# Turning q and k by 32 by 32 blocks on VectorE for seven of sixteen head pairs, with another order of the first loads' turns, in a fused BigBird attention and FNet kernel

## The chip, the cores and the metric

The kernel runs on one core of a Trainium2 chip. The metric is the device time of one execution in microseconds (us). TensorE is called PE here, VectorE DVE, ScalarE ACT, GpSimd POOL and SyncE SP, as the profile calls them; PEld is PE's loading of weights.

## What is computed

First comes block-sparse attention over 4 batches of 8 heads, 768 rows, head width 64, in float32. A row attends to its own 32-row block, the two neighbours, the first and last block, and three random blocks. Then, per batch, a Fourier mix and a two-layer network with 512 and 2048 channels:

```python
scores = scale * np.matmul(q, k.transpose(0, 1, 3, 2))     # masked by 32 x 32 blocks
attn = np.exp(scores - max) / sum
x = (attn @ v), heads side by side                          # (4, 768, 512)
mixed = np.real(np.fft.fft(np.fft.fft(x, axis=1), axis=2))
u = x + mixed
un = (u - mean) / np.sqrt(var + 1e-6)
out = u + np.maximum(un @ w_ch1, 0.0) @ w_ch2
```

## The kernel before

**Pairs, units, slots.** Heads are taken two at a time: 16 pairs (`n` = 0 to 15), four per batch. Both heads of a pair lie side by side on the 128 partitions (64 each) once q and k have been turned, so that the head's 64 columns are the contracted dimension. A pair has 12 units: 2 halves of the queries (384 rows each) by 6 tiles of 128 keys. A *slot* holds two units, so a pair has six slots, `s` = 0 to 5, and a batch (a *phase*) 24. `slot` writes down one slot: `scores` of its two units (four matrix products, L478), `weigh` (the exponential on ACT, L497, then the mask product on DVE, L499; in the first batch, phase 0, the mask is added on PE instead, L483, and ACT writes the weights itself, L494), then `values` of the units of the slot before (L522). From the second batch on, POOL adds up the weights (L509) and PE sums them over partitions once a pair (`total`, L583).

**Work of the mixer between the slots.** While batch b+1 is in attention, the Fourier mix and the network of batch b are placed between its slots; those of the last batch come after all slots. The network's first layer is done in `quad` (seven products of four matrix products each, L898), its second in `channels` (L954, "y" in the profile). The kernel keeps a small model of the time of each engine (`when`, `free`, `busy`, `give`) while it is being built, and `gap` places the next piece where that model says that its inputs are ready. Once it is built the order on every engine is fixed.

**Turning.** `load_q` and `load_k` bring a pair in with the rows on partitions. `turn` turns one half of q or k: PE transposes 128 by 128 pieces into the one PSUM bank of pool `ps_t` ("t"), four then two for q and three then three for k (L447, 12 per pair), and ACT copies them out (L450 for k, six copies and then three for q, L456, which also put q's rows into the order that the Fourier mix wants). At the end ACT squares the raw tile and keeps the sum per partition (L462), from which `highest` later decides whether the safe path `general` must run. The same bank is used by `place` (the transposes `xt`, L540, copied by ACT, L541), by `total`, and by part of the mixer's transposes (`utp`, L823). `slot` appends the turns of pair n+1 to a list `short` at s = 1, 2 (q) and 4, 5 (k); `gap` takes them from it when the model says that they are ready, and a loop near the end of `slot` forces out what is left. Loads are issued on SP's queue: q of pair n+2 at s = 3, k of pair n+1 at s = 0, each into a single buffer.

**The start.** For pair 0 the copies of q's first half are shared between DVE and ACT in turn, those of the second half are DVE's. DVE also builds the mask tables (L232, L245) and rounds the float64 weights of the network to float32, one 512-column chunk at a time, with two ACT operations (L410, L413) and then five DVE operations (L414 to L422) each; `w_steps` asks for 1.42 chunks per slot in phase 0. `warm` issues products of the identity that keep PE running while the first data arrives.

Of the kernel before, what the change touches and what calls it, by code (L numbers as in the profile page):

```python
# [11 lines left out]
FP32 = mybir.dt.float32  # L12
# [6 lines left out]
ACT = mybir.ActivationFunctionType  # L19
# [45 lines left out]
           ((384, 64, 191, 64, 64, -1), (704, -128, 64, 63, 63, -1), (640, 127, 0, 1, 1, 1)))  # L65


def _rows(view, tile):

    got = []  # L70
    for t, p0, runs, jump, n, s0, step in _ORDER:
        if t != tile:
            continue
        at = view[s0:s0 + 1, :]
        row, col = list(at.ap[0])[0], list(at.ap[1])
        if jump > 0:
            got.append((p0, runs * n, bass.AP(tensor=at.tensor, offset=at.offset,
                                              ap=[[jump * row, runs], [step * row, n], col])))
            continue
        for r in range(runs):  # L80
            at = view[s0 + r * jump:s0 + r * jump + 1, :]
            got.append((p0 + r * n, n, bass.AP(tensor=at.tensor, offset=at.offset,
                                               ap=[[step * row, n], col])))
    return got
# [3 lines left out]
def kernel(  # L88
# [14 lines left out]
    nc = tc.nc  # L103

    B, H, S, D = q.shape
    DM = H * D
    FF = w_ch1.shape[1]
    P = 128
    C = S // P
    BLK = 32  # L110
# [10 lines left out]
    scale = 1.0 / float(D) ** 0.5  # L121
    KA = D + NB
    NP = H // 2
    LIMIT = 400.0

    const = ctx.enter_context(tc.tile_pool(name="const", bufs=1))

# [25 lines left out]
    peaks = const.tile([P, 2 * B * NP], FP32, name="peaks")  # L153

    ld = ctx.enter_context(tc.tile_pool(name="ld", bufs=1))
    ldv = ctx.enter_context(tc.tile_pool(name="ldv", bufs=2))
    tp_p = ctx.enter_context(tc.tile_pool(name="tp_p", bufs=2))
# [16 lines left out]
    when = {"PE": 0.0, "ACT": 0.0, "DVE": 0.0, "POOL": 0.0}  # L174
    free = {"m": [0.0, 0.0], "t": [0.0]}

    def busy(engine, us, after=0.0):
        when[engine] = max(when[engine], after) + us
        return when[engine]
# [13 lines left out]
    pairs = [(b, j) for b in range(B) for j in range(NP)]  # L193
    loaded, v_of = {}, {}

    def load_k(n, queue=None):

        b, j = pairs[n]
        kt = loaded.get((n, 1))
        if kt is None:  # L200
            kt = ld.tile([P, C, 2, D], FP32, tag="k", name="kr")
        for i in range(2):
            (queue or nc.sync).dma_start(out=kt[:, :, i, :],
                                         in_=k[b, 2 * j + i].rearrange("(p c) d -> p c d", p=P))
        loaded[n, 1] = kt

    def load_q(n):

        b, j = pairs[n]
        qt = loaded.get((n, 0))  # L210
        if qt is None:
            qt = loaded[n, 0] = ld.tile([P, T, 2, 2, D], FP32, tag="q", name="qr")
        for t in range(T):
            for i in range(2):
                rows = q[b, 2 * j + i][2 * P * t:2 * P * (t + 1), :]
                nc.sync.dma_start(out=qt[:, t, :, i, :],
                                  in_=rows.rearrange("(p r) d -> p r d", r=2))
# [36 lines left out]
    def bit(n):  # L254
# [6 lines left out]
                                  ap=[[0, NB], [1, 2 * NB * NR]]))  # L261
# [3 lines left out]
    def warm(n):  # L265

        m = ps_m.tile([P, P], FP32, tag="m", name="warm")
        for _ in range(n):
            nc.tensor.matmul(m, ident, ident, start=True, stop=True)
# [163 lines left out]
    def turn(n, a, half):  # L433

        t = loaded[n, a]
        if half == 0:
            turned[n, a] = tp_p.tile([P, S], FP32, tag="qk"[a] + "T", name="qk"[a] + "T")
        dst = turned[n, a]
        first = n == 0 and half == 0
        tag, pool = ("m", ps_m) if first and a == 0 else ("t", ps_t)  # L440
        tp, at = pool.tile([P, 512], FP32, tag=tag, name="tp"), bank(tag)
        if a == 0:
            parts = [t[:, c // 2, c % 2, :, :] for c in (range(4, 6) if half else range(4))]
        else:
            parts = [t[:, T * half + c, :, :] for c in range(T)]
        for c, part in enumerate(parts):
            nc.tensor.transpose(tp[:, c * P:(c + 1) * P], part, ident)  # L447
        done = busy("PE", 0.15 * len(parts)) + HOP
        if a == 1:
            nc.scalar.copy(out=dst[:, half * HS:(half + 1) * HS], in_=tp[:, 0:HS])  # L450
            give(at, busy("ACT", 0.5, done))
        else:
            for i, (to, to_jump, frm, jump, cnt, step) in enumerate(_TURNED[half]):
                on, copy = (("DVE", nc.vector.tensor_copy) if n == 0 and (half == 1 or i % 2 == 0)
                            else ("ACT", nc.scalar.copy))
                copy(out=_grid(dst, to, 2, to_jump, cnt, 1),  # L456
                     in_=_grid(tp, frm, 2, jump, cnt, step))
                end = busy(on, 0.27 if cnt > 1 else 0.18, done)
            give(at, end)
        if half == 1:  # L460
            flat = t.rearrange("p t r i d -> p (t r i d)" if a == 0 else "p c i d -> p (c i d)")
            nc.scalar.activation(out=flat, in_=flat, func=ACT.Square,  # L462
                                 accum_out=peaks[:, 2 * n + a:2 * n + a + 1])
            busy("ACT", 1.05)

    UP = 2 * C
    UNITS = len(pairs) * UP
# [709 lines left out]
    def slot(sl):  # L1177
        phase, r = divmod(sl, SB)
        n, s = divmod(sl, SP)
        units = range(SLOT * sl, SLOT * sl + SLOT)  # L1180
        if sl < B * SB:
            for u, ps in [(u, scores(u)) for u in units]:
                weigh(u, ps)
        if not late:
            gap(1.5)
        if 0 < sl <= B * SB:
            done = [u - SLOT for u in units]
            for u in done:
                values(u)
            if phase == 0 or sl == SB:  # L1190
                add_up(done)
            for u in done:
                e_of.pop(u)

        reuse = n % NP == 0 and phase >= 2
        if sl > 0 and s == (5 if reuse else 3) and sl <= B * SB:
            b, j = pairs[n]
            at = oT_at[n, 0]
            if reuse:
                until(lambda: (b - 2, 0) in finished)  # L1200
                at = when["PE"] + LEAVES
            short.append(("t", at, lambda: place(n, 0)))
        if 0 < sl <= B * SB and s == 0 and n % NP != 1:
            short.append(("t", oT_at[n - 1, 1], lambda: place(n - 1, 1)))
        if sl < B * SB and n % NP == 1 and s == 1:
            b = pairs[n - 1][0]
            at = oT_at[n - 1, 1]
            if b >= 2:
                until(lambda: (b - 2, 1) in finished)
                at = when["PE"] + LEAVES  # L1210
            short.append(("t", at, lambda: place(n - 1, 1)))
        if sl > SB and s == 0 and sl <= B * SB:
            short.append(("t", acc_at[n - 1, 1], lambda: total(n - 1)))
        if n + 1 < len(pairs):
            for at, a, half in ((1, 0, 0), (2, 0, 1), (4, 1, 0), (5, 1, 1)):
                if s == at:
                    short.append(("t", 0.0, lambda a=a, half=half: turn(n + 1, a, half)))
            if s == 1:
                load_v(n + 1)
        if sl == 0:  # L1220
            short.append(("t", 0.0, lambda: turn(0, 1, 1)))
        if sl == 1:
            short.append(("t", 0.0, lambda: turn(0, 0, 1)))
        if phase == 0 and 4 <= sl < 4 + 2 * C:
            short.append(("m", 0.0, lambda: mask_step(sl - 4)))
        if r == 1 and 0 < phase:
            begin(phase - 1)
        left = SB * (phase + (0 if r == 0 else 1)) + 1 - sl
        us = sum(step[1] for step in late)
        pace = max(LEAST, min(MOST, (us - COVER) / left)) if left > 0 else MOST  # L1230
        state["owed"] = min(state["owed"], pace) + pace if late else 0.0
        gap(max(state["owed"], 0.0))
        while late and state["owed"] >= late[0][1] / 2:
            state["owed"] -= late[0][1]
            channel_step()
            gap(max(state["owed"], 0.0))

        while short and (s in (2, 5) or len(short) > 1 or phase == 0 or sl == B * SB):
            short.popleft()[2]()
        if s == 3 and n + 2 < len(pairs):  # L1240
            load_q(n + 2)
        if s == 0 and 0 < n < len(pairs) - 1:
            load_k(n + 1)
        w_loads()
        w_steps(sl)
        if sl >= 4 and sl % 2 == 0:
            table_step()
# [21 lines left out]
    state["got"] = 2  # L1269
    turn(0, 1, 0)  # L1270
    turn(0, 0, 0)
    warm(3)
    spread_q(keep_q[0:NB, :], keep)
    w_loads()
    for sl in range(B * SB + 1):
# [112 lines left out]
```

## Time and profile before

| What | Value |
| --- | --- |
| median of 4 runs | 1112.35 us (1110.98 to 1114.01) |
| the profiled execution's own time | 1111.01 us |
| its span | 1109.3 us |
| PE busy | 1067.5 us, 96% of the span |
| DVE busy | 664.7 us, 60% |
| ACT busy | 393.8 us, 36% |
| POOL busy | 274.2 us, 25% |
| mean granted PE clock | 0.994 |

The span is the time from the first to the last instruction in the trace; the execution's own time is 1.7 us more. A share of busy time is a mean over stages that have different limits, so the stages are read one by one. In this profile a product of 32-bit numbers stands as two matrix products, so "s x8" is the four score products of one slot. A timeline gives start, duration, engine, line, output and inputs, number of instructions, and in brackets how long the engine had been idle and what ended that.

The attention of the four batches lies at 9 to 133 us, 133 to 249 us, 249 to 576 us and 576 to 825 us. The last two hold long stretches (about 272 to 447 us and 605 to 703 us) in which the mixer has PE for itself. From 825 us on only the last batch's mixer is left.

### The profile page before, as it was taken

The numbers are of one execution on the slowest core, as the hardware profiler recorded it, in microseconds if no ns is written. First come the engines' busy times: TensorE is split into PE (matmuls) and PEld (weight loads), VectorE is DVE, ScalarE is ACT, GpSimd is POOL, SyncE is SP. The second block draws the span as 40 slices with busy tenths as digits, with TensorE's granted clock in tenths as the row PEclk, the third lists the DMA queues.
The fourth block names the chain that finished last, engine by engine and source line by source line (L and its number), as shares of the span: only waits on it lengthen the run. The fifth ranks groups of instructions, "written<-read, shape, count | busy, mean of one in ns | idle before, by whom it ended". The sixth has DMA issues, their size and how long they took to land.

```text
span 1109.3 us, 12468 instructions
## 1 busy us (share of the span) xinstructions
PE 1067.5 (96%) x4446; PEld 544.6 (49%) x4446; DVE 664.7 (60%) x1216; ACT 393.8 (36%) x818; POOL 274.2 (25%) x302
## 2 busy tenths in 40 slices
PE   8999988998899999999999999999999999999996
PEld 3333333544455545444444555454444555568675
DVE  5888878497754525653459355544356446575563
ACT  6788755555212102353443212244330202120210
POOL 1000088688100001255537000344540000000000
PEclk9999999999999999999999999999999999999999
DMA  7757311011000000211110000111000000100001
GB/s 219 209 176 214 94 50 43 15 45 42 1 1 1 0 1 19 66 32 28 43 29 15 1 0 1 51 50 29 1 1 0 1 1 19 39 1 1 1 16 44
DMA packets 65187, 44.30 MB, mean 40 GB/s; under 512 B 52814, under 2 KB 57948, under 8 KB 65116
## 3 DMA queue, kind: packets, MB, share of 16 engines
q1 hardware_dynamic: 63228, 42.62, 13.7%
q10 hardware_dynamic: 1856, 0.79, 0.3%
q8 instruction: 37, 0.61, 0.2%
q14 instruction: 34, 0.28, 0.1%
q0 software_dynamic: 32, 0.01, 0.0%
HBM read 37.11 MB, written 6.29 MB: 39 GB/s over the span
## 4 chain that ended last, share of the span: by engine, by line
PE 86%; DVE 8%; ACT 3%; issue 2%; POOL 0%; ACTq 0%; DVEq 0%; POOLq 0%
PE y L954 23%; PE z L898 15%; PE s L478 11%; PE o L522 9%; PE yp L898 7%; PE yy L1017 6%; PE xp L898 4%; DVE e L499 2%; PE tp L447 2%; PE zp L711 1%; PE sp L569 1%; PE xt L540 1%; PE zp L682 1%; PE s L483 1%; PE utp L823 1%
## 5 line engine op out<-in xcount | busy, mean ns | idle before, releaser
L509 POOL TENSOR_TENSOR acc<-acc,e 128x384 f32<-128x384 f32 x192 | 198.3, 1066 | 90.6 <-DVE e L499 90.1
L499 DVE TENSOR_TENSOR e<-s,mask 128x768 f32<-128x768 f32 x144 | 131.2, 951 | 78.4 <-ACT s L497 78.0
L478 PE MATMUL s<-qT,kT 64*128 64x384 f32 x768 | 161.6, 526 | 9.3 <-DVE e L499 7.4
L522 PE MATMUL o<-e,vr 128*64 128x384 f32 x768 | 145.1, 499 | 0.0
L497 ACT ACTIVATE s<-s 128x768 f32<-128x768 f32 x144 | 109.2, 794 | 65.4 <-PE s L478 64.6
L957 DVE TENSOR_TENSOR x<-y,x 128x512 f32<-128x512 f32 x72 | 49.7, 691 | 133.9 <-PE y L954 133.8
L954 PE MATMUL y<-w_sb,hB 128*128 128x512 f32 x288 | 128.4, 595 | 1.1 <-DVE x L957 1.0
L954 PE MATMUL y<-w_sb,hA 128*128 128x512 f32 x288 | 128.8, 594 | 0.6 <-ACT zs L713 0.6
L509 POOL TENSOR_TENSOR acc<-e 128x384 f32<-128x384 f32 x48 | 51.8, 1100 | 231.3 <-DVE e L499 173.1
L903 DVE TENSOR_TENSOR hA<-z,hA 128x384 f32<-128x384 f32 x64 | 35.7, 558 | 111.5 <-PE z L898 111.5
L478 PEld LDWEIGHTS s<-qT,kT 64*128 64x128 f32 x768 | 63.1, 187 | 68.8 <-DVE e L499 25.2
L898 PE MATMUL z<-unT,t 128*128 128x384 f32 x256 | 93.0, 486 | 0.0
L774 POOL TENSOR_SCALAR st<-st 128x1 f32<-128x1 f32 x24 | 6.6, 276 | 344.5 <-DVE st L773 344.1
L954 PEld LDWEIGHTS y<-w_sb,hB 128*128 128x128 f32 x288 | 53.3, 190 | 64.7 <-issue 62.1
L522 PEld LDWEIGHTS o<-e,vr 128*64 128x64 f32 x768 | 46.6, 136 | 73.9 <-issue 71.4
L954 PEld LDWEIGHTS y<-w_sb,hA 128*128 128x128 f32 x288 | 52.9, 190 | 59.6 <-issue 56.6
L907 ACT ACTIVATE hA<-hA 128x384 f32<-128x384 f32 x64 | 33.4, 522 | 123.7 <-DVE hA L903 123.1
L898 PEld LDWEIGHTS z<-unT,t 128*128 128x128 f32 x256 | 48.6, 190 | 33.9
L907 ACT ACTIVATE hB<-hB 128x384 f32<-128x384 f32 x64 | 33.5, 523 | 85.7 <-DVE hB L903 85.7
L898 PE MATMUL z<-t,w_sb 128*128 128x384 f32 x128 | 48.0, 499 | 3.1 <-DVE t L860 3.1
L898 PE MATMUL xp<-unT,w_sb 128*128 128x384 f32 x128 | 47.1, 491 | 1.5 <-ACT zs L713 1.1
L898 PE MATMUL yp<-unT,w_sb 128*128 128x384 f32 x128 | 46.7, 487 | 0.2 <-DVE un L747 0.2
(190 smaller groups left out, 1394.9 us busy)
## 6 DMA issues: line engine op xcount, KB each, us to landing
wraw<-in_moe_w_ch_dram SPq DMA_DIRECT2D x32, 512.0 KB
qr<-in_q_dram SPq DMA_DIRECT2D x90, 64.0 KB
vr<-in_v_dram SPq DMA_DIRECT2D x30, 192.0 KB
kr<-in_k_dram SPq DMA_DIRECT2D x28, 192.0 KB
out_dram<-x SPq DMA_DIRECT2D x16, 128.0 KB
out_dram<-x SPq DMA_DIRECT2D x8, 256.0 KB
out_dram<-x SPq DMA_DIRECT2D x8, 126.0 KB
out_dram<-x SPq DMA_DIRECT2D x4, 252.0 KB
```

Of the source, the lines that this page charges most:

```text
L447: nc.tensor.transpose(tp[:, c * P:(c + 1) * P], part, ident)
L478: nc.tensor.matmul(s[:, i, 0:HS], kT[D * i:D * i + D, c * P:(c + 1) * P], qT[D * i:D * i + D, half * HS:(half + 1) * HS], start=True, stop ...
L497: nc.scalar.activation(out=s[:, :, 0:HS], in_=s[:, :, 0:HS], func=ACT.Exp, scale=scale)
L499: nc.vector.tensor_tensor(out=e, in0=s[:, :, 0:HS], in1=m.broadcast_to([P, 2, HS]), op=ALU.mult)
L509: nc.gpsimd.tensor_add(out=acc, in0=e_of[u - 1][:, i, :] if c == 1 else acc, in1=e[:, i, :])
L522: nc.tensor.matmul(o[D * i:D * i + D, :], vt[:, i, c, :], e[:, i, :], start=(c == 0), stop=(c == C - 1))
L898: nc.tensor.matmul(to, a[:, k, :], c[:, k, :], start=(k == 0), stop=(k == ND // 2 - 1))
L903: tt(out=to, in0=ps, in1=a, op=ALU.add)
L907: nc.scalar.activation(out=h, in_=h, func=ACT.Relu)
L954: nc.tensor.matmul(y, hs[0, half][:, l, m * P:(m + 1) * P], w2_sb[:, 4 * r + l, :], start=(l == 0), stop=(l == 3))
L957: nc.vector.tensor_tensor(out=x[:, m, :], in0=y, in1=x[:, m, :], op=ALU.add)
L1017: nc.tensor.matmul(ps, a[:, k, :], c[k // 2][:, k % 2, :] if isinstance(c, list) else c[:, k, :], start=(k == 0), stop=(k == 3))
```

## The change

For pairs 9 to 15 (`n >= BY_VECTOR`, 2*4+1) `turn` is no longer called. Four transfers per tensor (32 partitions each, runs of 32 numbers) load q and k so that each partition holds, for one of 32 rows in a block, that row's 32 columns of all 24 blocks. VectorE then transposes all 32 by 32 blocks of the 128 by 768 tile in one instruction: q in place, k straight into the order of its tiles (a step of 512 bytes between neighbouring writes, six of them, and then the next column). ACT squares the raw tiles as before (q's before the transpose, with its output thrown into the tile that will hold the turned q) and puts q's rows in order with six copies. These steps have fixed places at the end of a slot: s = 0 squares of q, 1 transpose of q, 2 copies of q, 4 transpose of k, 5 squares of k.

In the start, all copies of q's first half for pair 0 go to ACT, `warm(3)` becomes `warm(7)`, and the second half of q of pair 1 is appended at s = 3 instead of 2. The loop that forces out what is left in `short` now takes items that the model holds to be ready first, and stops when there is none, except in some slots. The threshold of the check on the sums of squares goes from 400 to 200.

```diff
+_IN_ORDER = ((0, 129, (256, 127, 2), (64, -128, 2), (1, 2, 64)),
+             (129, 259, (63, -257, 2), (1, 2, 63)), (128, 0, (127, 257, 2)),
+             (384, 639, (256, -127, 2), (64, 128, 2), (1, -2, 64)),
+             (513, 509, (63, 257, 2), (1, -2, 63)), (512, 384, (127, 127, 2)))
+
+def _at(ap, start, dims):
+    at = ap[:, start:start + 1]
+    return bass.AP(tensor=at.tensor, offset=at.offset,
+                   ap=[list(at.ap[0])] + [list(d) for d in dims])
...
-    LIMIT = 400.0
+    LIMIT = 200.0
...
+    BY_VECTOR = 2 * NP + 1
+
+    def load_blocks(n, a, tile):
+        b, j = pairs[n]
+        for i in range(2):
+            rows = (q, k)[a][b, 2 * j + i].rearrange("(t r) (g d) -> g r t d", r=BLK, d=BLK)
+            for g in range(D // BLK):
+                p0 = D * i + BLK * g
+                nc.sync.dma_start(
+                    out=tile[p0:p0 + BLK, :].rearrange("r (t d) -> r t d", d=BLK), in_=rows[g])
+        loaded[n, a] = tile
+
     def load_k(n, queue=None):
+        if n >= BY_VECTOR:
+            load_blocks(n, 1, ld.tile([P, S], FP32, tag="k", name="kb"))
+            return
...
     def load_q(n):
+        if n >= BY_VECTOR:
+            load_blocks(n, 0, ld.tile([P, S], FP32, tag="q", name="qb"))
+            return
...
-                on, copy = (("DVE", nc.vector.tensor_copy) if n == 0 and (half == 1 or i % 2 == 0)
+                on, copy = (("DVE", nc.vector.tensor_copy) if n == 0 and half == 1
                             else ("ACT", nc.scalar.copy))
...
+    def squares(n, a):
+        t = loaded[n, a]
+        if a == 0:
+            turned[n, 0] = tp_p.tile([P, S], FP32, tag="qT", name="qT")
+        nc.scalar.activation(out=t if a else turned[n, 0], in_=t, func=ACT.Square,
+                             accum_out=peaks[:, 2 * n + a:2 * n + a + 1])
+        busy("ACT", 1.05)
+
+    def flip_blocks(n, a):
+        t = loaded[n, a]
+        out = t
+        if a == 1:
+            kT = turned[n, 1] = tp_p.tile([P, S], FP32, tag="kT", name="kT")
+            out = _at(kT, 0, [(1, P), (P, C)])
+        nc.vector.transpose(out=out, in_=t)
+        busy("DVE", 1.0)
+
+    def in_order(n):
+        t = loaded[n, 0]
+        qT = turned[n, 0]
+        for to, frm, *dims in _IN_ORDER:
+            nc.scalar.copy(out=_at(qT, to, [(d[0], d[2]) for d in dims]),
+                           in_=_at(t, frm, [(d[1], d[2]) for d in dims]))
+        busy("ACT", 1.7, when["DVE"])
...
-            for at, a, half in ((1, 0, 0), (2, 0, 1), (4, 1, 0), (5, 1, 1)):
-                if s == at:
+            for at, a, half in ((1, 0, 0), (2 if n > 0 else 3, 0, 1), (4, 1, 0), (5, 1, 1)):
+                if s == at and n + 1 < BY_VECTOR:
                     short.append(("t", 0.0, lambda a=a, half=half: turn(n + 1, a, half)))
...
-        while short and (s in (2, 5) or len(short) > 1 or phase == 0 or sl == B * SB):
-            short.popleft()[2]()
+        while short and (s in (2, 5) or len(short) > 1 or phase == 0 or r == 0):
+            ready = [i for i in short if max(i[1], min(free[i[0]])) <= when["PE"] + 0.1]
+            if not ready and s not in (2, 5) and r > 0:
+                break
+            item = ready[0] if ready else short[0]
+            short.remove(item)
+            item[2]()
+        if BY_VECTOR <= n + 1 < len(pairs):
+            for at, fn, args in ((0, squares, (n + 1, 0)), (1, flip_blocks, (n + 1, 0)),
+                                 (2, in_order, (n + 1,)), (4, flip_blocks, (n + 1, 1)),
+                                 (5, squares, (n + 1, 1))):
+                if s == at:
+                    fn(*args)
...
-    warm(3)
+    warm(7)
```

## The prediction

> **What bounds the kernel now.** I read the shares of busy time first, then each engine's busy time by stage (cut where the slots begin), then every idle stretch of PE in the timeline.
>
> ```profile
> PE 1067.5 (96%) x4446; PEld 544.6 (49%) x4446; DVE 664.7 (60%) x1216; ACT 393.8 (36%) x818; POOL 274.2 (25%) x302
> ```
>
> The stages, as length, then PE, PEld, DVE, ACT and POOL busy:
>
> ```profile
> 9.00:133.30 124.30, 119.91 (x742) 42.47 (x742) 99.14 (x219) 98.66 (x202) 0.00 (x0) 1.00 0.62 185
> 133.30:248.80 115.50, 104.11 (x569) 45.85 (x568) 89.41 (x124) 65.61 (x142) 84.28 (x82) 0.98 0.17 42
> 248.80:283.00 34.20, 28.07 (x149) 12.98 (x149) 26.33 (x35) 16.84 (x34) 27.62 (x31) 0.95 0.14 36
> ...
> 447.30:604.90 157.60, 156.38 (x676) 71.78 (x675) 89.88 (x120) 67.23 (x141) 77.84 (x75) 1.00 0.14 36
> ...
> 702.60:822.00 119.40, 118.48 (x504) 54.09 (x503) 59.51 (x88) 47.95 (x96) 50.90 (x52) 1.00 0.09 26
> ```
>
> Where pairs 10 to 15 are turned (447 to 822 us), PE idles 1% and DVE half; only 133 to 283 us is not PE-bound, there PE waits for DVE. What a turn takes on PE is read from starts, not durations (0.27 us each, overlapping). A slot with a second-layer product, of 6.84 us:
>
> ```profile
> 778.19 1.56 PE L478 MATMUL s<-qT,kT 64*128 64x384 f32 x8
> 779.68 1.51 PE L522 MATMUL o<-e,vr 128*64 128x384 f32 x8
> 781.12 0.55 PE L447 MATMUL tp<-ident,kr 128*128 128x128 f32 x3
> 781.50 3.60 PE L954 MATMUL y<-w_sb,hB 128*128 128x512 f32 x8
> 785.03 1.24 PE L478 MATMUL s<-qT,kT 64*128 64x384 f32 x6
> ```
>
> Three transposes push the product back by 0.38 us. Likewise four take 0.53 (720.86 to 721.39) and two 0.27 (724.32 to 724.59). Slots with nothing of the mixer are close to a loop of score, exponential, mask product, next score:
>
> ```profile
> 473.92 1.82 DVE L499 TENSOR_TENSOR e<-s,mask 128x768 f32<-128x768 f32 x2 [1.40 <-ACT s L497]
> ...
> 475.16 1.56 PE L478 MATMUL s<-qT,kT 64*128 64x384 f32 x8
> ...
> 478.41 1.78 PE L478 MATMUL s<-qT,kT 64*128 64x384 f32 x8 [0.25 <-DVE e L499]
> ```
>
> Such a slot lasts 3.25 us with 0.25 us of waiting, so a transpose taken out of it returns little; but DVE idles 1.4 us ahead of its mask products, and a new operation fits there.
>
> [...] the subtraction of L860 takes 0.68 us alone and 1.48 beside POOL's additions. [...] if it does, it costs some 0.8 us more (1.48 less 0.68). [...] a read stepping by 24 bytes (L238) took 0.841 us for 768 columns[...].
>
> **The change part by part**, against the profiled 1111.01 us (span 1109.3; 1.7 lie around it). The order is that of the changed kernel as built, the durations are those of before.
>
> *Transposes removed.* Pairs 9 to 15: 7 x (0.53 + 0.27 + 0.38 + 0.38) = 10.9 us. With them go two waits of PE for the one bank: 1.12 us at 264.03 (for ACT's copies of q) and 0.73 at 702.11 (for its copy of k). Sum 12.8. Taken off: 0.5 for three turns in mixer-free slots (474.8, 547, 563) that the loop keeps; and half of the 2.3 us of pair 9 at 258 to 272 us, 1.15, since that stretch ends in PE waiting 3.10 us for DVE at 282.94. Net -11.1.
>
> *DVE.* 14 transposes of 0.95 us, 13.3 us in a stretch where DVE has over 100 us idle. Each stands after the slot's last addition and ahead of the next slot's two mask products, behind which the next scores and values wait. Ahead of those DVE idles 1.40 us (473.92), 1.58 (507.82), 1.80 (483.90): covered. For q I take 0.95 (ends 0.95 and 1.75); for k 1.2 (ends 0.95 and[...] 3.3). I charge 0.7 us for the odd collision.
>
> *ACT.* A pair loses 1.53 us of q copies and 0.96 of k copies and gains six copies, by the rows of like size (0.37, 0.28, 0.17, twice) at most 1.64; the squares stay. ACT is under half busy there: 0.
>
> *DMA.* Per pair q's six issues (3.8 us of SP's queue) and k's two (1.2) become four each, of 768 short runs like k's now (0.6 to 1.0 us each). SP's order is otherwise kept: v's loads and the stores stand behind them. q now goes out at 476.62 and crosses in about 5.5 us at a DMA share under a half; twice the runs may take 11. Need comes 16 us or more after issue (q: s = 3 to the next s = 0; k: s = 0 to s = 4): 0. Without that cover ACT's square, and behind it the exponentials, would stall.
>
> *Place moves.* In phase 0 the `xt` transposes move behind the next slot's scores: their waits for ACT's oT (0.83 at 60.16, 0.97 at 107.12, 1.00 at 122.97) and 0.31 at 48.88 go; new is a back-to-back turn of k of pair 1, waiting about 0.5. Net -2.6. Elsewhere: `total` now follows `xt` in pair 8 and `xt` follows `total` in pair 12 on the same bank, +0.6 and +0.2 (0.85 as at 837.60, less today's 0.62 at 583.80); phase 1 loses waits of 1.34 and 0.64 and gains one of 1.12, -0.4 in a DVE-bound stage. Net +0.4.
>
> *The start.*
>
> ```profile
> 9.18 0.92 PE L478 MATMUL s<-qT,kT 64*128 64x384 f32 x4 [1.71 <-ACT qT L456]
> ...
> 18.11 0.44 PE L447 MATMUL tp<-ident,qr 128*128 128x128 f32 x2 [1.12 <-ACT qT L456]
> ...
> 20.65 0.43 DVE L414 TENSOR_SCALAR wraw<-wraw 128x512 uint32<-128x512 uint32 x1 [1.51 <-ACT wraw L413]
> ...
> 23.29 0.92 PE L478 MATMUL s<-qT,kT 64*128 64x384 f32 x4
> ```
>
> With all six copies on ACT (1.03 us as a group, from 6.9) q is ready by 8.0; the seven warm products, from 6.63 at 0.11 us a half, end at 8.2: scores start 1.0 us earlier. Slot 2 then starts at 15.8. But the second half of q, whose PE part moves behind slot 2's scores, is copied by DVE, and there it now stands behind two weight chunks. ACT reaches those at 17.05 and the first DVE step starts at 18.3; two chunks take 5.96 (20.65 to 26.61 today), the copies 0.56: 24.8. Slot 3 needs q whole: it starts at 24.9 instead of 23.29, though PE is free at 20.5. That is +1.6, and +0.3 for the second turn of q of pair 1, done before slot 3 today and after it then: +1.9.
>
> Sum: -11.1 + 0.7 - 2.6 + 0.4 + 1.9 = -10.7, profiled time 1100.3. The runs' median is 1.3 above the profiled one, so 1101.6 us.
>
> **Rivals.** *Half of it:* transposes at the dear ends (q 1.75, k 3.3). k then exceeds its 1.6 us of cover by 1.7 in some four light slots (6.8 less what the next wait absorbs): about 5 lost, 1106.6. For it: no strided write is in the trace; against: the 0.841 us row. *Slower:* k's transpose stalls the loop. Beyond 1.6 us of cover in four light slots and some 4 in three slots with products, a cost T loses 4(T - 1.6) + 3(T - 4); that eats 10.7 at T = 4.2 us. At 6 us (over six times the mask product) it is 23.6, hence 1124. *It returns nothing in attention:* the loop of 3.25 us rules every slot; then only phase 0 and the two bank waits remain, -2.6 - 1.85 + 0.4 + 1.9 + 0.7 = -1.5, 1110.9. Against: the slot of 6.84 us above is full of PE.
>
> **How the numbers follow.** Forecast 0.60 (own range 1098 to 1105), half 0.16, slower 0.14, nothing 0.10. I call 0.2% (2.2 us) what a measurement can tell from no change: the first two are faster, of the third all slower, and "nothing" is split 0.04 faster, 0.06 same. So 0.80, 0.06, 0.14. The range 1096 to 1112 leaves out the slower case and about 0.05 below.
>
> **What would show it.** Right: PE's transposes down by 84; slots like 778.19's at about 6.45; new DVE rows near 0.95 and 1.2 us; no `xt` waits for oT in phase 0; an idle of about 4 us on PE before slot 3's scores, ended by a DVE copy of q. Wrong: a k row over 2 us with waits of PE's scores for the mask product behind it; ACT's squares waiting for q's transfer; new waits of PE for DVE in the mixer's own stretches, whose order at 605 to 703 us also changes.

## The result and the profile after

The changed kernel takes 1109.39 us (median of 42 executions, 1106.56 to 1111.5), the kernel before 1111.26 us (63 executions, 1108.3 to 1117.21). The ratio is 0.9983, with a 95% interval of 0.9976 to 0.9991: faster by about 1.9 us, where 10.7 were forecast. The profiled execution of the changed kernel took 1107.8 us with a span of 1106.0, against 1111.01 and 1109.3: 3.3 us less in the span. It is among the quicker third of its executions.

The block transposes are there, and about as cheap as forecast. Groups of instructions by line of the changed kernel (line, engine, operation, output <- input, count; then busy us, mean ns of one; then idle time ahead of them):

```profile
L517 DVE STREAM_TRANSPOSE kT<-kb 128x768 f32<-128x768 f32 x7 | 10.6, 1517 | 0.0
L517 DVE STREAM_TRANSPOSE qb<-qb 128x768 f32<-128x768 f32 x7 | 6.8, 968 | 0.0
L525 ACT COPY qT<-qb 128x256 f32<-128x256 f32 x14 | 6.0, 426 | 0.9 <-DVE qb L517 0.9
```

q costs 0.97 us of VectorE (0.95 forecast, as much as the mask product of 768 columns, L499, with 0.951 in the trace of before), k 1.52 (1.2 forecast, bounds 0.95 and 3.3; the trace of before shows neither 1.2 nor 3.3). ACT's six copies (426, 308 and 195 ns for 256, 126 and 2 columns, each twice) sum to 1.86 us a pair, not "at most 1.64". Nothing waits for the new transfers: ACT's squares (L507) and the transposes, which read them, have 0.0 us of idle ahead of them.

Where did the time go, then? A slot is two units of attention, six slots to a pair, 24 to a phase; its start on PE is that of its first score product. The start of every slot, read from both timelines (one execution each) and subtracted, shows where one kernel gains on the other:

| slot | before, us | changed minus before, us |
|---|---|---|
| 2 | 18.47 | -2.70 |
| 3 | 23.29 | +1.40 |
| 4 | 28.22 | +4.69 |
| 6 (pair 1) | 38.60 | +5.97 |
| 24 (phase 1) | 133.30 | +2.76 |
| 48 (phase 2) | 248.78 | +3.93 |
| 72 (phase 3) | 575.91 | -2.87 |
| 95 (last) | 822.08 | -3.27 |

So from slot 48 on, where the block transposes are, the change returns 7.2 us in this execution, of which 1.3 turn out below to be chance. But it enters that stretch 3.9 us late, and slots 2 to 6 alone cost 8.7 us. PE's timeline of the changed kernel there (start, busy us, line, product, count; in brackets the idle time ahead and what ended it):

```profile
18.36 1.51 PE L585 MATMUL o<-e,vr 128*64 128x384 f32 x8
...
24.69 1.65 PE L541 MATMUL s<-qT,kT 64*128 64x384 f32 x4 [4.04 <-DVE qT L492]
...
28.71 2.83 PE L585 MATMUL o<-e,vr 128*64 128x384 f32 x8
...
32.91 0.98 PE L541 MATMUL s<-qT,kT 64*128 64x384 f32 x4
...
35.68 1.51 PE L585 MATMUL o<-e,vr 128*64 128x384 f32 x8
```

The stall is the forecast one: slot 3 at 24.69 us (24.9 predicted), PE idle 4 us, released by VectorE's copy of q. What was not forecast stands behind it. The same eight products `o` take 1.51 us before the stall, 2.83 after it and 1.51 again from 33 us on. Slot 3 to slot 4 takes 8.22 us, where the kernel before takes 4.93. VectorE's timeline shows what the copy stood behind: the last of two weight chunks.

```profile
23.39 0.69 DVE L458 TENSOR_TENSOR w_sb<-w_sb,wraw 128x512 f32<-128x512 f32 x1
24.00 0.55 DVE L492 COPY qT<-tp 128x128 f32<-128x128 f32 x3
```

The granted clock of PE, cut into stretches (columns: busy us and count of PE, PE weight loads, VectorE, ACT, POOL; then PE's clock as a share of full speed, DMA share, GB/s), says why the products were slow. First the kernel before, then the changed one:

```profile
24.60:33.00 8.40, 8.40 (x56) 2.89 (x54) 8.02 (x15) 7.16 (x14) 0.00 (x0) 1.00 0.70 185
```

```profile
24.60:33.00 8.40, 8.31 (x30) 2.30 (x30) 2.78 (x5) 3.03 (x5) 0.00 (x0) 0.50 0.66 180
```

In the 8.4 us behind the stall the clock is at 0.50: 30 products instead of 56 in the same time, with PE "busy" throughout. A busy share doesn't show such a loss.

Two later losses stand out. At slot 82 (735.31 us) the timeline of all engines of the changed kernel reads:

```profile
731.64 1.86 ACT L525 COPY qT<-qb 128x256 f32<-128x256 f32 x6
733.40 1.49 ACT L560 ACTIVATE s<-s 128x768 f32<-128x768 f32 x2
...
735.31 1.78 PE L541 MATMUL s<-qT,kT 64*128 64x384 f32 x8 [1.72 <-DVE e L562]
```

ACT comes out of the mixer's relus, does the six copies in one piece, and only then the exponentials that VectorE and PE wait for. And at slot 73 the transposes `xt` stand right behind `total`'s product `sp` and wait for VectorE to empty it:

```profile
578.31 0.52 PE L603 MATMUL xt<-ident,oT 128*128 128x128 f32 x3 [1.42 <-DVE sums L616]
```

### The profile page after: what moved, and what is told of

Same layout as the page of the kernel before. It is cut to its first block, busy times and chain, and to the rows that moved or that the text cites. A ratio compares the mean times of both kernels' runs of the same rounds, so it can differ in the third digit from the quotient of the medians.

```text
span 1106.0 us, 12273 instructions
## 1 busy us (share of the span) xinstructions
PE 1062.7 (96%) x4370; PEld 536.3 (48%) x4370; DVE 670.1 (61%) x1227; ACT 389.7 (35%) x786; POOL 271.3 (25%) x302
## 4 chain that ended last, share of the span: by engine, by line
PE 84%; DVE 9%; ACT 2%; issue 2%; POOL 1%; DMA 1%; ACTq 0%; DVEq 0%; POOLq 0%
PE y L1017 23%; PE z L961 14%; PE s L541 10%; PE o L585 9%; PE yp L961 7%; PE yy L1080 6%; PE xp L961 3%; DVE e L562 3%; PE zp L774 1%; PE sp L632 1%; PE zp L745 1%; DMA out_dram<-x 1%; PE s L546 1%; PE xt L603 1%; PE tp L483 1%
## 5 line engine op out<-in xcount | busy, mean ns | idle before, releaser
L541 PE MATMUL s<-qT,kT 64*128 64x384 f32 x768 | 163.3, 528 | 15.0 <-DVE e L562 10.7
L981 ACT COPY hA<-xp 128x384 f32<-128x384 f32 x32 | 15.3, 479 | 95.7 <-PE xp L961 95.7
```

What stands on the lines that cost most here:

```text
L541: nc.tensor.matmul(s[:, i, 0:HS], kT[D * i:D * i + D, c * P:(c + 1) * P], qT[D * i:D * i + D, half * HS:(half + 1) * HS], start=True, stop ...
L981: nc.scalar.copy(out=h11, in_=x)
```

## The experiments

The theory called START below is that the transposes return what they were to return and the start gives it back. The rival, BLOCKS, is that the transposes and the new order of turns are themselves worth only 2 to 3 us. All medians are of executions on the same chips as the kernel before (1111.2 to 1111.3 us in each group).

### The second half of q ahead of the weight chunks

```diff
-            if not ready and s not in (2, 5) and r > 0:
+            if not ready and s not in (2, 5) and sl > 1 and r > 0:
```

> The changed kernel with the second half of q of pair 0 turned in slot 1 again, ahead of the two weight chunks on VectorE; all else as changed. Theory START (the gain of the block transposes is given back by PE's stall before slot 3 and by what follows it: PE at half speed for 8 us, then phase 1): the 4.04 us wait of slot 3's scores for DVE's qT is gone, slot 4 starts near 27.5 to 28.5 us instead of 32.91, and the kernel takes 4 to 6 us less than the changed one, 1103.5 to 1105.5. Rival BLOCKS (the transposes themselves and the new order of turns cost what is missing; the start is caught up with later by PE's waits for DVE in phase 1): within 1 us of the changed kernel, 1108.5 to 1110.5.

Measured: 1105.4 us, ratio 0.9957 (0.994 to 0.9974), 4.0 us under the changed kernel. Slot 4 starts at 27.64 us. PE's timeline, in which the old wait of 1.12 us ahead of q's second half is back and no other, has slots 3 and 4 at full speed:

```profile
22.71 0.92 PE L541 MATMUL s<-qT,kT 64*128 64x384 f32 x4
...
27.64 0.92 PE L541 MATMUL s<-qT,kT 64*128 64x384 f32 x4
```

The start was worth 4 us; BLOCKS, which had no change here, is out as the whole story. The lead over the changed kernel, 6.2 us at slot 6, is 5.7 at slot 48 and 4.1 at the end.

### The block transposes alone

The start, the copies and the order of phase 0 are those of the kernel before; as in the changed kernel, `short` is still emptied at the first slot of a phase, so the wait at slot 73 stays:

```diff
...
-            ready = [i for i in short if max(i[1], min(free[i[0]])) <= when["PE"] + 0.1]
-            if not ready and s not in (2, 5) and r > 0:
-                break
-            item = ready[0] if ready else short[0]
-            short.remove(item)
-            item[2]()
+            short.popleft()[2]()
...
-    warm(7)
+    warm(3)
```

> The kernel before with the block transposes of pairs 9 to 15 alone: start and order of phase 0 as before (the queue of short work is still emptied at the first slot of a phase's quarter). START: 7 to 8 us below the kernel before, about 1103.5 to 1104.5, since phases 2 and 3 keep their 7.2 us. BLOCKS: 2 to 3 us below it, about 1108.5.

Measured: 1107.52 us, ratio 0.9971 (0.9955 to 0.9988): 3.7 us, between the two theories and nearer to BLOCKS. In its trace slots 48 to 95 return 5.8 us (+1.17 to -4.63), not 7.2, and 1.05 is lost at slots 27 and 28. There the order and PE's idles (0.86 and 1.12 us) are those of the kernel before, but not the speed. PE's timeline before:

```profile
148.14 1.56 PE L478 MATMUL s<-qT,kT 64*128 64x384 f32 x8
```

and with the block transposes alone:

```profile
148.37 2.93 PE L541 MATMUL s<-qT,kT 64*128 64x384 f32 x8
```

So START overrated the transposes: slots 48 to 95 return 5.8 us and not 7 or 8, and a dip in speed at slot 27 takes 1.05 of it away.

### The start and the order alone

```diff
-    BY_VECTOR = 2 * NP + 1
+    BY_VECTOR = len(pairs)
```

> The changed kernel without any block transpose (all pairs turned on PE): only the start and the order in which short work is taken. START: 2 to 4 us above the kernel before, 1113.5 to 1115.5, with the stall before slot 3 and pair 8 starting near 252 us. BLOCKS: 0 to 2.6 us below it, 1108.7 to 1111.3, as the place moves gain 2.6 in phase 0.

Measured: 1114.26 us, ratio 1.0039 (1.0022 to 1.0055): 3.0 us slower than before, as START has it. Slot 6 is 6.17 us late. The rival's gain of 2.6 in phase 0 is real (6.17 falls to 2.95 at slot 24) but smaller than the loss ahead of it, and phase 1 loses 2.55 again: slot 48 is 5.50 late and the last one 5.44.

### PE kept busy in the stall

17 products of the identity that nobody reads, and then nine:

```diff
     def slot(sl):
+        if sl == 3:
+            warm(17)
```

> The changed kernel with 17 more products of the identity (about 3.8 us, used by nobody) on PE between slot 2 and slot 3's scores: the stall for VectorE stays, PE just isn't idle in it. If idling is what makes PE slow afterwards: slot 3 still starts near 24.7 us, its four score products take 0.92 us instead of 1.65, slot 4 starts about 4.6 us after it (29.3) instead of 8.2, and the kernel takes about 3 us less than the changed one, 1106. If the slow PE has another cause (the weight chunks' transfers, VectorE or ACT being late): slot 4 still about 8 us after slot 3, 1109 to 1110.

> The changed kernel with 9 products of the identity instead of 17 between slot 2 and slot 3's scores: PE is busy for about 2 us and then idle for about 2.2, instead of idle for 4.4. [...] slot 3's scores take 0.92 us for four, slot 4 starts 4.5 us after slot 3, and the kernel takes what it takes with 17, 1108.6. If a shorter idle is enough: slot 3 to slot 4 takes 6 to 8.2 us, and the time is that of the changed kernel, 1109.4.

This takes away the idling and leaves the stall. PE's timeline with 17 products:

```profile
20.96 4.06 PE L305 MATMUL warm<-ident 128*128 128x128 f32 x34
25.07 0.92 PE L541 MATMUL s<-qT,kT 64*128 64x384 f32 x4
...
29.52 0.92 PE L541 MATMUL s<-qT,kT 64*128 64x384 f32 x4
```

and with nine, idle for the rest:

```profile
21.81 2.27 PE L305 MATMUL warm<-ident 128*128 128x128 f32 x18
25.92 0.92 PE L541 MATMUL s<-qT,kT 64*128 64x384 f32 x4 [1.83 <-DVE qT L492]
...
30.37 0.92 PE L541 MATMUL s<-qT,kT 64*128 64x384 f32 x4
```

Slot 3 to slot 4 takes 4.45 us in both, against 8.22. The slow PE came from idling; the weights' transfers, VectorE and ACT were as late as in the changed kernel (VectorE's copy of q starts at 24.37 and 25.23 us, there at 24.00). An idle of 1.83 us did no harm here, one of 4.04 us did; the last section has equal idles with either outcome. The whole kernel gains less than the 3 us expected: 1108.63 us (ratio 0.9974, 0.9965 to 0.9983) and 1107.67 (0.9974, 0.9965 to 0.9983), so 0.8 and 1.7 us under the changed one, with intervals that overlap its own. With 17, the lead of 3.4 us at slot 4 is down to 0.3 at slot 48: in phase 1 PE waits for VectorE, and its clock was 0.89 from 133 to 150 and 0.73 from 150 to 156 us.

### k transposed without its order

```diff
-            out = _at(kT, 0, [(1, P), (P, C)])
+            out = kT
```

> The changed kernel with k's seven transposes written contiguously: the placement of k's columns into its tiles is left out, so scores of pairs 9 to 15 are those of another order of k. What the strided write costs: the row falls from 1517 to about 970 ns. If k's transpose is hidden in VectorE's idle time, as the prediction has it: within 0.7 us of the changed kernel, 1108.7 to 1109.5. If VectorE's time is on the path: 7 x 0.55 = 3.8 us less, 1105.6.

Groups by line of this kernel:

```profile
L517 DVE STREAM_TRANSPOSE kT<-kb 128x768 f32<-128x768 f32 x7 | 6.8, 967 | 0.0
```

The scattered write costs 0.55 us a transpose (1517 less 967 ns). It is hidden: the kernel took 1109.88 us (ratio 0.9989, 0.9977 to 1.0002), no faster than the changed one and just above the range expected for a hidden cost. From slot 53 to slot 81, where four of the seven k are turned, it gains 3.86 us on the kernel before, the changed kernel 3.97.

### The second half of q copied by ACT

The turn stays where the change put it:

```diff
-                on, copy = (("DVE", nc.vector.tensor_copy) if n == 0 and half == 1
+                on, copy = (("DVE", nc.vector.tensor_copy) if False
```

> The changed kernel with the three copies of the second half of q of pair 0 on ACT instead of VectorE, where the turn stands now (behind slot 2's scores). If only the queue on VectorE made slot 3 late: no idle over 1 us ahead of slot 3, which starts near 20.6 us (2.7 earlier than before's 23.29, 2.1 earlier than with the copies first), and the kernel takes 1103.4, 2 us less than with the copies first. If phase 1, which waits for VectorE, takes up what the start gives: the same as with the copies first, 1105.4. If ACT's copies come late behind its weight steps: slot 3 at 23 us or later, no better than 1105.4.

Measured: 1102.9 us, ratio 0.9929 (0.9917 to 0.9942), 6.5 us under the changed kernel and 2.5 under the one with the copies first (intervals that barely overlap). ACT makes the copies at 20.26 us, between two activations, and PE hardly waits:

```profile
20.86 0.92 PE L541 MATMUL s<-qT,kT 64*128 64x384 f32 x4 [0.35 <-ACT qT L492]
```

VectorE's queue alone made slot 3 late, and most of what is saved at the start is kept to the end. Slot 6 starts 2.06 us ahead of the kernel before, and slot 95 9.14 ahead.

### ACT's six copies in two parts

On top of the kernel with the copies first, the second three copies move to the end of slot s = 3:

```diff
...
-                                 (2, in_order, (n + 1,)), (4, flip_blocks, (n + 1, 1)),
+                                 (2, in_order, (n + 1, 0)), (3, in_order, (n + 1, 1)), (4, flip_blocks, (n + 1, 1)),
```

> The kernel with q's copies first in the start, and ACT's six copies that order q split: three at the end of slot s = 2 as now, three a slot later. If the six in one group are what makes slot 82's exponentials late (1.7 us): that slot's wait for DVE's e goes, and the kernel takes 1.5 to 2 us less than the one with the start mended alone, 1103.6. If the two relus or the output copy ahead of them do it: no change, 1105.4.

The timeline at slot 82:

```profile
730.17 0.97 ACT L525 COPY qT<-qb 128x256 f32<-128x256 f32 x3
...
732.96 1.78 PE L542 MATMUL s<-qT,kT 64*128 64x384 f32 x8 [0.84 <-DVE e L563]
```

Half the copies, half the wait: 0.89 us of copies and 0.88 of waiting went. So the copies delay PE one for one there, but the expected "goes" was too much. The time itself, 1104.85 us (ratio 0.9928, 0.9909 to 0.9947), doesn't stand clear of the 1105.4 without the split.

### Total and place apart

With that split, only one of `total` and `place` is taken at the first slot of a phase:

```diff
...
-        while short and (s in (2, 5) or len(short) > 1 or phase == 0 or r == 0):
+        must = s in (2, 5) or (s == 1 and n % NP == 0) or sl == B * SB
+        while short and (must or len(short) > 1 or phase == 0):
...
-            if not ready and s not in (2, 5) and r > 0:
+            if not ready and not must and r > 0:
```

> The same as the split kernel, and at the first slot of a phase's quarter only one of place and total is taken, the other a slot later, as in the kernel before. If the xt transposes right behind total on the one bank cost what slot 73 lost (1.9 us at once, 0.8 after the next slot): 0.8 to 1.9 us less than the split one, about 1102.5. If the slots after it take that up: no change, 1103.6.

Measured: 1102.82 us, ratio 0.9917 (0.9904 to 0.9929), 2.0 us under the split alone, with intervals that overlap, so that the slots have to tell the two apart. PE's timeline ahead of slot 74:

```profile
577.66 0.55 PE L604 MATMUL xt<-ident,oT 128*128 128x128 f32 x3 [0.55 <-DVE r L663]
```

The wait of 1.42 us behind `sp` is gone and one of 0.55 stands a slot later. Over slots 72 to 77 that is 0.6 us more gained than with the split alone, over slots 48 to 53, in the other phase that has both at its first slot, 0.95.

### All three together

The copies by ACT, the split and the order of total and place together, the last with one word more, so that the first pair's turns stay where the change put them:

```diff
-        must = s in (2, 5) or (s == 1 and n % NP == 0) or sl == B * SB
+        must = s in (2, 5) or (s == 1 and n > 0 and n % NP == 0) or sl == B * SB
```

> The changed kernel with all three mends: the second half of q of pair 0 copied by ACT, ACT's six ordering copies split three and three, and only one of place and total taken at the first slot of a phase's quarter (but for the first pair). If the three losses are separate, they add up: the start as with ACT's copies (pair 8 at about 245 us, 1102.9 in all), less 0.9 at slot 82 and 0.8 to 1.2 at the quarters: 1100.8 to 1101.3, that is what the prediction had for the change (10 us below the kernel before). If phase 1's waits for VectorE and the clock's dips take one of them back: 1102 to 1103.

Measured: 1101.55 us, ratio 0.9917 (0.99 to 0.9933), 9.7 us under the kernel before and 7.8 under the changed one. Its profiled execution took 1100.34 us. It is the fastest kernel run here, though its interval overlaps that of the one with nothing but ACT's copies, 1.35 us above it.

Slot starts minus those of the kernel before, us, from the timelines of one execution each. Seven of the kernels here share the changed start up to slot 2, and slot 2 starts at 15.62 to 16.99 us in their traces, so differences of up to 1.4 us between columns can be the executions' own:

| slot | changed | copies first | 17 products | copies by ACT | blocks alone | start alone | all three |
|---|---|---|---|---|---|---|---|
| 3 | +1.40 | -0.58 | +1.78 | -2.43 | 0.00 | +2.51 | -1.97 |
| 4 | +4.69 | -0.58 | +1.30 | -2.54 | -0.01 | +4.95 | -2.08 |
| 24 | +2.76 | -3.42 | -0.69 | -5.29 | +0.03 | +2.95 | -4.82 |
| 48 | +3.93 | -1.79 | +3.63 | -3.74 | +1.17 | +5.50 | -3.52 |
| 72 | -2.87 | -6.98 | -1.57 | -10.34 | -4.24 | +5.24 | -8.91 |
| 95 | -3.27 | -7.37 | -1.97 | -9.14 | -4.63 | +5.44 | -10.78 |

## Why the prediction was wrong

It had the sign and the stall, and missed the size: 10.7 us forecast, 3.3 in the profile's span. By its own steps, the start and phase 0 came out 3.5 us worse than forecast, phase 1 1.6 and phases 2 and 3 2.4.

*The start, the step that failed.* "That is +1.6, and +0.3 for the second turn": slot 3 came out at +1.40 in this trace (+2.41 and +2.51 with k plain and with the start alone, whose slot 2 began 1.0 and 1.1 us later), so VectorE's queue was read right. But the step priced an idle PE at the length of the idle only. The clock fell behind it, and slot 4 lost another 3.3 us, which the two kernels with products in the stall show by losing none of it. The prediction wrote down "an idle of about 4 us on PE" and did not ask what such an idle does. In the trace the clock is 0.50 from 22.84 to 33.08 us, three times 3.41; why it lasted so long isn't shown, as PE was busy throughout the last two (3.42 and 3.41 us). In medians of the whole kernel, the two with products get only 0.8 and 1.7 us of it back; the one with the copies first, which has no stall, takes 4.0 us less. A further 1.2 us went between slots 5 and 6, in the turns of pair 1, where 0.8 were allowed (0.3 in this step, 0.5 in the next).

*Place moves in phase 0: right.* -2.6 forecast: 3.1 us of waits that go, and a new one of 0.5 that is counted above. The waits are gone, and slots 6 to 24 return 3.2 us.

*Phase 1.* -0.4 forecast, +1.2 measured. That is about the clock again, 0.50 from 152.54 to 155.96 us: behind idles of 0.87 and 1.12 us the scores of slot 27 take 2.36 us instead of 1.56, and slot 28 starts 1.3 us later than it would. That the block transposes alone lose 1.05 at the same place, with the order of the kernel before, shows that it isn't the order; the last section shows what it went with.

*Transposes removed: -11.1 was too much.* "What a turn takes on PE is read from starts" counted the gap between the transpose's start and the product behind it. But here a product that starts behind transposes is itself shorter from start to next start. PE's timelines of one slot, first of the kernel before:

```profile
781.12 0.55 PE L447 MATMUL tp<-ident,kr 128*128 128x128 f32 x3
781.50 3.60 PE L954 MATMUL y<-w_sb,hB 128*128 128x512 f32 x8
```

and then of the changed one:

```profile
775.48 1.56 PE L541 MATMUL s<-qT,kT 64*128 64x384 f32 x8
...
778.41 3.70 PE L1017 MATMUL y<-w_sb,hB 128*128 128x512 f32 x8
782.04 1.56 PE L541 MATMUL s<-qT,kT 64*128 64x384 f32 x8
```

From its first score product to the next slot's the slot goes from 6.84 (778.19 to 785.03) to 6.56 us (775.48 to 782.04): 0.28, not the 0.38 read from the transposes' starts, as `y` now takes 0.1 us longer. Likewise four return 0.44 at slots 55 and 67 rather than 0.53 (0.2 at slots 61 and 85), and two 0.18 at slots 62 and 86 rather than 0.27. A pair is then worth 1.18 us instead of 1.56, so seven are worth 2.7 us less than the sum had. The prediction's mark of "about 6.45" for this slot was the same error.

*The two bank waits.* The one at 264.03 is gone. The one at 702.11 only changed its owner: in the changed kernel `xt` waits 0.68 us at 698.75 for ACT to empty the same bank of a transpose of the mixer. Worth 0 instead of 0.73.

*ACT: "0" was wrong.* Under half busy on average, ACT was late at slot 82 by the length of the copies: 1.76 us lost, 0.88 with half of them. The step asked how busy ACT is and not what stands behind the copies.

*`xt` behind `total`.* Priced at 0.2 for pair 12; at once it cost 1.93 us, of which the next slot returned 1.17. Taking it away was worth 0.6.

*VectorE and DMA: right.* 0.7 us were charged for VectorE and, by the run with cheaper k transposes, about nothing was needed; the transfers stayed hidden. As the 0.95 taken for q had it (its other bound, 1.75, adds the 0.8 us that the subtraction of L860 loses beside POOL), its transposes didn't wait for POOL: 965 to 972 ns with POOL's additions beside them (at 263.4 and 584.5 us) or without (at 762.7). k's scattered write cost 0.55 us for 768 columns.

The terms of phases 2 and 3 don't close. The misses found (2.7, 0.7, 1.8 and 0.4) sum to 5.6 us, less 0.7 for VectorE is 4.9, and the gap is 2.4. Most of the difference lies in slots 48 to 53, which returned 3.5 us where about 1.7 were forecast (1.12 and 1.15, less 0.6), and 1.3 to 1.4 us more than with the copies first or with the blocks alone. That surplus is luck of the clock. Both traces have an idle of 2.17 us ahead of slot 48, and behind it the kernel before ran slowly, the changed one at full speed:

```profile
248.78 2.93 PE L478 MATMUL s<-qT,kT 64*128 64x384 f32 x8 [2.17 <-DVE e L499]
```

```profile
252.71 1.78 PE L541 MATMUL s<-qT,kT 64*128 64x384 f32 x8 [2.17 <-DVE e L562]
```

With the copies first and with the blocks alone these scores take 2.93 and 2.78 us, and slot 48 lasts 7.73 and 7.85 us instead of 6.42. Less this 1.3, the changed kernel's 7.2 is near their 5.6 and 5.8. The other 1.2 us stay open.

## What to carry to other kernels

When a change makes the matmul engine wait, price the wait and then the clock behind it (here 0.50 for 10.24 us, with 4.04 us of wait): read the granted clock of the stretch, and where the wait can't go, a few products that nobody reads may be cheaper in it than nothing (0.8 us with 17 and 1.7 with nine, though with overlapping intervals). Compare two kernels slot by slot only after looking whether the clock was the same in both. Short idles close together can bring the clock down as a long one does: 0.86 and 1.12 us ahead of slot 27 were followed by 3.41 us at 0.50 with the block transposes alone. Before moving a copy to another engine's queue, list what that queue holds at that moment, for a queue with much idle time on average can be the late one where it counts (VectorE's, busy for 61% of the span, reached q's copy at 24.00 us). Price the removal of a small operation from start to next start of the whole slot, since its neighbours can lengthen when it goes (`y` by 0.1 us here).

## What the hardware showed

- PE's granted clock went with how busy PE was in fixed steps of 3.41 us, not with the length of one idle. In the traces of the kernel before and of the changed one it stands at 1.00 or 0.50, and all its changes within a trace lie whole steps of 3.41 us apart. Cut there, the two traces have 634 steps at full clock with another behind them. All seven in which PE was busy (as the profile models it) for less than 0.45 of the step were followed by one at half clock, none of the 621 above 0.56 was, and one of the six between was (busy for 0.475; the five at 0.496 to 0.557 were not). The steps lie elsewhere in each of the two (one starts at 146.23 us in the kernel before, at 145.72 in the changed one), so the same idles can have either outcome. These are steps around the idles of 0.87 and 1.12 us ahead of slot 27 (length, PE busy and count, clock, DMA share, GB/s), first of the kernel before, then with the block transposes alone:

```profile
142.81:146.23 3.42, 2.55 (x17) 1.00 0.00 0
146.23:149.64 3.41, 2.29 (x16) 1.00 0.02 5
```

```profile
144.34:147.75 3.41, 1.43 (x10) 1.00 0.00 0
147.75:151.16 3.41, 3.41 (x10) 0.50 0.02 5
```

In the first the idles are spread over two steps, in the second they fall into one, as in the changed kernel (1.62 us busy from 149.13 to 152.54 us, then 0.50). At the matching place, 144.54 to 147.95 us, the kernel before has the same 1.43 us busy, but its steps don't start there. With these two idles the scores of slot 27 took 1.56 us with nine products too. Behind the 2.17 us ahead of slot 48 they took 1.78 us in the changed kernel and with all three together, 2.93 in the kernel before and with total and place apart, and 2.82 with nine products; behind 1.72 or 1.73 us at slot 82, 1.78 in the changed kernel and with nine products, 2.43 with k plain and 2.04 with the copies by ACT. With nine products in the stall the clock was 1.00 from 15 to 33 us, with the idle of 1.83 us in it; an estimate from 1.83 and 3.41 us is that this idle inside one step would leave 0.46 of it busy, near the 0.475 that was followed by half clock and the 0.496 that was not.
- Much of the spread between executions goes with this. Among the changed kernel's, the five with a mean granted clock of 0.993 took 1106.56 to 1106.95 us, the 26 with 0.988 or less 1108.87 to 1111.5.
- A 32 by 32 block transpose of 128x768 in f32 takes 0.97 us on VectorE in place and 1.52 us when each next column is written 512 bytes on.
